# Top-k attention and a feed-forward block on one core: scores made two units ahead and set around the value products, loads spread, one transfer for the values

## The chip, the cores and the metric

The kernel runs on one core of a Trainium2 chip. The metric is the device time of one execution in microseconds (us); lower is better. The time of a kernel is the median of its runs. A profile shows one execution, on five engines: PE (TensorE, matrix products and transposes; its weight loads are listed as PEld), DVE (VectorE), ACT (ScalarE), POOL (GpSimd) and SP (SyncE, which issues nearly all transfers here). Each engine works through its own list of instructions in order.

## The reference

For 8 batches and 8 heads, 576 queries and keys of 64 numbers each, the 32 largest scores of each query are kept, and a softmax over them weighs the values. The heads are put side by side into rows of 512, and a block of layer norm, a hidden layer of 2048 with ReLU and a residual follows.

```python
scores = scale * np.matmul(q, k.transpose(0, 1, 3, 2))          # (8, 8, 576, 576)
kth = np.partition(scores, -top_k, axis=-1)[..., -top_k:-top_k + 1]
mask = scores >= kth
scores = np.where(mask, scores, -1000000000.0)
attn = np.exp(scores - np.max(scores, axis=-1, keepdims=True))
attn = attn / (np.sum(attn, axis=-1, keepdims=True) + 1e-09)
x = heads_side_by_side(np.matmul(attn, v))                      # (8, 576, 512)
xn = (x - mu) / np.sqrt(var + 1e-06) * g_ln
out = x + np.maximum(xn @ w_ch1, 0.0) @ w_ch2                   # 512 -> 2048 -> 512
```

Everything is float32, but the weights come as float64 and are turned into float32 on the chip.

## The kernel before

**Jobs, groups, units.** A job is a pair of heads of one batch with some of their query tiles; a unit is one tile of 128 queries for both heads (two tiles of scores, 128x576 each), or, for the last 64 queries, one "rest" unit that holds both heads in one tile. There are 160 units, counted from 0. Batch 0 has jobs of two units and then four jobs with the rest unit alone (units 0 to 19); batch 1 has four jobs of two and four of three (20 to 39). From batch 2 on, each batch has 20 units: four jobs of three units (two tiles and the rest unit) and then four jobs of two. So jobs of three end with units 42, 45, 48, 51, then 62, 65 and so on, jobs of two with 53, 55, 57, 59, then 73 and so on. The four jobs of three are the first of their heads in the batch: they load q and k and turn them. The jobs of two fetch the turned tiles that were kept in HBM.

**Steps.** All instructions are issued in the order in which one loop writes them down (`for n in range(END)`, one step for each unit); nothing reorders them. In step n, with n above 8:

- `scores(x)` (L386 on PE, evacuated by ACT, L367) for the units that `due(n)` names: n+1 up to step 16, both in step 17, n+2 after that. Their tile `sc` has 5 buffers.
- `values(g)` (L600, L607): the value products of a group whose last unit is n-3. They need `pt`, the turned weights (one buffer), the values `vb`, and a tile `ends` for the 64 keys of each head that do not fill a block of 128.
- `select(u, 0)` to `select(u, 3)` on DVE: four rounds of finding the 8 largest (L421, L429) and taking them out (L415); between the second and the third stand `halve` of unit n+1 (L407, L408), which needs its scores, and in some steps `turn_heads` (L316).
- `prepare` and `watch` of unit n-1 on POOL (L452, L444, L445): the threshold.
- `mask` of unit n-1: ACT (L481), then a subtraction on POOL (L484). `weigh` of unit n-2: the exponential on ACT (L492), the first of the two ahead of the step's copies of scores.
- The weights of unit n-2 are turned into `pt`: by PE (L546, L575), or, from unit 40 on for every unit that is neither a rest unit nor the last of its group, by `move`: two transposes on DVE (L524), a store `turned` to HBM (L529) and four loads into `pt` (L532), which wait for the store's landing. `move` stands at the very end of the step, after `select(u, 3)`.
- `load_values`, near the end of the step after a job's last unit: four transfers on SP, two into `vb` (L301) and two into `ends` (L305). `ends` are two tiles, zeroed once, for jobs in turn.
- `load`, right after `turn_heads`: eight transfers of q and k on SP (L289) in one go.
- `fill()`, eight times in a step, puts in products of the feed-forward block (L745, L902), as many as an even share over the steps asks for; it counts a tick that the class `Later` uses to put work off.

Tiles for scores, turned weights, value products and other brief results share five PSUM buffers of one pool (`brief`, tag "ps").

```python
        ahead = [] if n == 0 else [n + 1] if n < CONVERTING else [n + 2]
        if n == CONVERTING:
            ahead = [n + 1, n + 2]
        return [units[i] for i in ahead if i < N]
```

Of the kernel before, what the change touches and what calls it, by code (L numbers as in the profile page):

```python
# [11 lines left out]
FP32 = mybir.dt.float32  # L12
# [9 lines left out]
J = 4  # L22
# [7 lines left out]
def compute(  # L30
# [12 lines left out]
    nc = tc.nc  # L43
    P = nc.NUM_PARTITIONS
    B, H, S, D = q.shape
# [3 lines left out]
    JP = J * P  # L49
    R = S - JP  # L50
# [6 lines left out]
    def pool(name, bufs, **kw):  # L57
        return ctx.enter_context(tc.tile_pool(name=name, bufs=bufs, **kw))

    NV = 2  # L60
# [6 lines left out]
    vpool = pool("v", NV)  # L67
# [23 lines left out]
    def const(shape, name):  # L91
        return consts.tile(shape, FP32, tag=name, name=name)
# [9 lines left out]
        return mmps.tile([P, 512], FP32, tag="mm", name=name)  # L102


    ends = [const([P, P], f"ends{i}") for i in range(NV)]
    for t in ends:
        nc.gpsimd.memset(t[:], 0.0)
    if doubt is not None:
        watched = const([P, 34], "watched")
        nc.gpsimd.memset(watched[:], -1.0)  # L110
# [88 lines left out]
    queue = list(pieces)  # L199
# [5 lines left out]
    def weights(n, phase):  # L205

        now, before = batches.get(n, []), batches.get(n - 1, [])
        if phase == 0:  # L210
            for x in batches.get(n + 1, []):
                x.fetch()
            for x in now[0::2]:
                x.split()
        elif phase == 1:
            for x in before:
                x.join()
            for x in now[1::2]:
                x.split()
# [10 lines left out]
    def pop():  # L230
        kind, cost, run, may = todo.pop(0)
        assert not may or may()
        owed[0] -= cost
        run()
# [24 lines left out]

    sums_later, ends_later, stores = Later(), Later(), Later()  # L260

    def fill(least=0):
        tick[0] += 1
        ends_later.settle(END_AGE)
        fetch_forms(FETCH_AGE)
        owed[0] = min(owed[0] + share[0], 6.0)
        while todo and (not todo[0][3] or todo[0][3]()):
            if owed[0] < todo[0][1] / 2 and least <= 0:
                break
            least -= 1  # L270
            pop()
# [7 lines left out]
            self.b, self.hp = b, hp  # L279
            self.groups = groups  # L280

    def load(job, first, second):

        job.ins = {}
        for name, src, queue in (("k", k, first), ("q", q, second)):
            t = ldpool.tile([P, S], FP32, tag=name + "in", name=name + "in")
            for i in range(P // 32):
                head, d0 = 2 * job.hp + i * 32 // D, i * 32 % D
                queue.dma_start(  # L289
                    t[i * 32 : (i + 1) * 32, :].rearrange("b (n a) -> b n a", a=32),  # L290
                    src[job.b, head, :, d0 : d0 + 32].rearrange("(n b) a -> b n a", b=32),
                )
            job.ins[name] = t

    def load_values(job):
        vb = vpool.tile([P, 2 * J, D], FP32, tag="v", name="vb")
        job.ends = ends[jobs.index(job) % NV]
        for hh in range(2):
            rows = v[job.b, 2 * job.hp + hh]
            k0, end = (0, JP) if hh == 0 else (R, 0)  # L300
            nc.sync.dma_start(  # L301
                vb[:, hh * J : (hh + 1) * J, :],
                rows[k0 : k0 + JP, :].rearrange("(c p) d -> p c d", p=P),
            )
            nc.sync.dma_start(  # L305
                job.ends[hh * R : (hh + 1) * R, hh * D : (hh + 1) * D],
                rows[end : end + R, :],
            )
        job.v = vb

    def turn_heads(job):
        job.T = {}
# [48 lines left out]
    def scores(u):  # L361

        u.sc = scpool.tile([P, 2, S], FP32, tag="sc", name="sc")
        made = [score_half(u, s) for s in range(2)]
        for t in range(len(u.tiles)):
            for s in range(2):
                nc.scalar.copy(  # L367
                    u.sc[:, t, s * HALF : (s + 1) * HALF], made[s][t][:, 0:HALF]
                )
# [148 lines left out]
    def move(u):  # L518

        i0 = place_of(u)  # L520
        ni = P // 32
        blocks = u.sc[:].rearrange("p t n -> p (t n)")[:, 0 : 2 * JP]
        for t in range(2):
            nc.vector.transpose(  # L524
                blocks.rearrange("p (j t c n) -> p j t c n", j=ni, t=2, c=J)[:, :, t],
                u.e[:, t, t * R : t * R + JP].rearrange("p (c j k) -> p j c k", c=J, k=32),
            )
        hbm = hbmpool.tile([P, 2 * JP], FP32, tag="turned", name="turned")
        nc.sync.dma_start(hbm[:], blocks)  # L529
        for j in range(ni):  # L530
            to = u.group.pt[j * 32 : (j + 1) * 32, 0 : 2 * J].rearrange("k c n -> k (c n)")
            nc.sync.dma_start(  # L532
                to[:, i0 * 2 * P : (i0 + ni) * 2 * P].rearrange("k (i x) -> k i x", i=ni),
                hbm[:, j * 2 * P : (j + 1) * 2 * P].rearrange("(i k) x -> k i x", k=32),
            )
# [59 lines left out]
    def values(g):  # L595
        vb = g.job.v
        av = brief("av")
        for c in range(J):
            for h in range(2):
                nc.tensor.matmul(  # L600
                    av[h * D : (h + 1) * D, 0 : g.nq],
                    vb[:, h * J + c, :],
                    g.blocks[:, h, 0 : g.nq // 32, c, :],
                    start=(c == 0),
                    stop=False,
                )
        nc.tensor.matmul(  # L607
            av[:, 0 : g.nq], g.job.ends[:], g.pt[:, 2 * J, 0 : g.nq],
            start=False, stop=True,
        )  # L610
        g.av = av
# [316 lines left out]
            )  # L928

    PER_ROW = 1.71e-3  # L930
    SUM_AGE, END_AGE, FETCH_AGE, STORE_AGE = 7, 6, 10, 8
    blocks = []
    plain_done, formed, used, fetched = [None], [None], [], [0]

# [41 lines left out]
    def fetch_forms(age):  # L976
        if done(formed[0]):
            free = 4 + sum(tick[0] - x >= age for x in used)
            while fetched[0] < min(free, 8 * (len(blocks) - 1)):
                fetch_form()  # L980
# [11 lines left out]
    jobs = []  # L992
# [7 lines left out]
    units = []  # L1000
# [7 lines left out]
    N = len(units)  # L1008
    END = N + 6

    fresh = []
# [8 lines left out]
    CONVERTING = max(n for n in batches if batches[n]) + 2  # L1020
    EARLY = jobs[NHP].first
# [16 lines left out]
    for j in jobs:  # L1038
        if j.hp == NHP - 1:
            b = j.b  # L1040
            step = j.last + (3 if j.last < EARLY else 4)
# [28 lines left out]
    def after(n):  # L1070

        turned = at(n - 1) if n - 1 < EARLY else at(n - 2) if n - 2 >= EARLY else None
        last = at(n - 2) if n - 2 < EARLY else at(n - 3) if n - 3 >= EARLY else None
        return turned, last.group if last and last is last.group.units[-1] else None

    def due(n):

        ahead = [] if n == 0 else [n + 1] if n < CONVERTING else [n + 2]  # L1080
        if n == CONVERTING:
            ahead = [n + 1, n + 2]
        return [units[i] for i in ahead if i < N]

    DVE_UNIT = 6.0 + 1.65 * low_rounds
    DVE_REST, DVE_MOVE, DVE_TURN = 0.58 * DVE_UNIT, 1.4, 1.45
# [3 lines left out]
    for j in jobs[1:]:  # L1090
        before = jobs[jobs.index(j) - 1]
        made = next(n for n in range(N) if units[j.first] in due(n))
        step = min(before.first, made - 1)
        if j.twin:
            fetches.setdefault(max(step - 1, 0), []).append(j)
        else:
            turns[step] = j
            keeps[step + 1] = j
# [43 lines left out]
                    left += sum(b.cost() for b in gives[m])  # L1142
        return max(0.0, even) / SLOTS

    recips, rows_of = {}, {}
    pairs_left, made_pair = list(range(4)), []

    def arrived(n, key, x):
# [19 lines left out]
    for n in range(END):  # L1168
# [9 lines left out]
        ex, g = after(n)  # L1178
        g = g if g and not g.quick else None
# [7 lines left out]
        moved = ex is not None and ex.moved  # L1187

        if ex and not early:
            weigh(ex, 0)  # L1190
        for x in due(n):
            scores(x)
        if g:
            values(g)
        if u:
            select(u, 0)
        for j in fetches.get(n, []):
# [40 lines left out]
        if n in turns:  # L1238
            turn_heads(turns[n])
            later = fresh.index(turns[n]) + 1  # L1240
            if later < len(fresh):
                load(fresh[later], nc.sync, nc.sync)
        if not quick:
            weights(n, 1)
        fill()
        if mk and not early:
            mask(mk, 0)
# [9 lines left out]
            select(u, 2)  # L1257
        for blk, i in rows_of.pop(n, []):
            blk.stats(i)
        for blk in gives.get(n - 2, []):  # L1260
            blk.inverse()
        if last and ex.group.sums is not None:
# [12 lines left out]
        for x in (u if n < EARLY else None, mk if n > EARLY else None):  # L1275
            if x and x is units[x.job.last]:
                load_values(x.job)
        if quick:

            values(quick)  # L1280
            take_values(quick)
            for den in recips.pop(n + 1):
                nc.vector.reciprocal(den, den)
            place(quick)
            weights(n, 0)
            weights(n, 1)
        if u:
            select(u, 3)
            if u.i < CONVERTING:
                prepare(u)  # L1290
        if moved:
            move(ex)
        for x in (g, quick):
            if x and x.job.hp == NHP - 1:
                for qt in x.qts:
# [7 lines left out]
        if late and late.job.hp == NHP - 1:  # L1303
            r = late.job.b // 2
# [62 lines left out]
```

## Time and profile before

| | |
|---|---|
| median of 3 runs | 1657.19 us (1655.44 to 1660.09) |
| the profiled execution | 1655.4 us, of it 1653.6 us span of instructions |
| PE, DVE, ACT, POOL busy | 1508.0, 1334.3, 1067.4, 1078.1 us |
| granted clock of PE, mean | 0.963 of full speed |
| transfers | 211.5 MB, mean 128 GB/s |

The profile gives the busy time of each engine and its share of the span, the span in 40 slices of 41 us (each digit is the busy share in tenths, 9 for 90% or more; PEclk is the clock granted to PE in tenths), groups of instructions by line with their durations, and for idle time the instruction that ended it ("waited for"). "L386" is a line of the kernel before; the sequencer of SP is listed as SPq. A wait for several things is put down to the one that came last by the profile, and with transfers that share a semaphore the name can be that of a neighbour in the queue. The stretches of the batches: up to about 340 us the weights are converted and batches 0 and 1 run, then come the other batches, and from about 1500 us on only feed-forward products are left.

### The profile page before, as it was taken

To read this page: it belongs to the slowest core of one execution; us is meant where nothing else is said; L and a number is where in the kernel's file an instruction comes from. 1 tells how busy PE (TensorE), PEld (TensorE's weight loads), DVE (VectorE), ACT (ScalarE), POOL (GpSimd) and SP (SyncE) were. 2 spreads that over 40 slices of the span, in tenths; PEclk is the share of its full clock that TensorE was granted. 3 is DMA by queue.
4 is the path that set the end of the run, shared out by engine and by line. 5 is a ranking of instruction groups with operands and counts; after the bars stand their busy time and mean duration, and the time that the engine had idled before them with its cause. 6 is when DMAs were issued, how large, how long until landed. Compare 5 with 4: busy or idle time off the path is not lost. (4 is left out here: it accounts for less than half of the span.)

```text
span 1653.6 us, 27426 instructions
## 1 busy us (share of the span) xinstructions
PE 1508.0 (91%) x7898; PEld 1132.7 (68%) x7898; DVE 1334.3 (81%) x3990; ACT 1067.4 (65%) x2712; POOL 1078.1 (65%) x1607
## 2 busy tenths in 40 slices
PE   2557898999989899899999999999989999999997
PEld 1235546677757677677777776677767777778886
DVE  6878998788989898899998988799879999884000
ACT  5777966677757676567666765677656766654311
POOL 4667866867657475667675866576756676856433
PEclk9768999999989999999999999999999999999999
DMA  7433434321454354554655444545554445442211
GB/s 199 110 100 114 130 81 119 114 66 46 109 167 152 109 168 118 162 153 118 185 160 168 126 126 135 163 138 138 158 158 150 134 135 181 149 131 71 91 32 53
DMA packets 358951, 211.52 MB, mean 128 GB/s; under 512 B 250756, under 2 KB 331144, under 8 KB 358792
## 3 DMA queue, kind: packets, MB, share of 16 engines
q1 hardware_dynamic: 354056, 209.10, 43.8%
q8 instruction: 65, 1.06, 0.3%
q10 hardware_dynamic: 4736, 0.59, 0.2%
q14 instruction: 94, 0.77, 0.2%
HBM read 145.62 MB, written 63.96 MB: 127 GB/s over the span
## 5 line engine op out<-in xcount | busy, mean ns | idle before, releaser
L484 POOL TENSOR_TENSOR e<-e,sc 128x576 f32<-128x576 f32 x288 | 412.4, 1435 | 419.4 <-ACT e L481 403.1
L745 PE MATMUL hps<-xT,w 128*128 128x256 f32 x2304 | 548.2, 384 | 2.5 <-ACT xT L707 2.5
L745 PEld LDWEIGHTS hps<-xT,w 128*128 128x128 f32 x2304 | 422.0, 191 | 72.8 <-issue 16.7
L429 DVE MAX8 m<-hi 128x8 f32<-128x296 f32 (+1 forms) x1152 | 464.3, 444 | 1.1
L415 DVE MATCH_REPLACE8 hi<-m,hi 128x288 f32<-128x288 f32 (+1 forms) x864 | 378.2, 444 | 0.0
L902 PE MATMUL ops<-w,h 128*128 128x256 f32 x1360 | 324.8, 381 | 0.0
L902 PEld LDWEIGHTS ops<-w,h 128*128 128x128 f32 x1360 | 247.7, 190 | 40.4 <-issue 6.9
L492 ACT ACTIVATE e<-e,m 128x576 f32<-128x576 f32 x288 | 224.8, 780 | 52.8 <-POOL e L484 52.4
L407 DVE TENSOR_TENSOR hi<-sc 128x576 f32<-128x576 f32 (+1 forms) x160 | 120.1, 751 | 157.4 <-POOL watched L452 135.7
L481 ACT ACTIVATE e<-sc,m 128x576 f32<-128x576 f32 x288 | 223.9, 781 | 14.6 <-POOL m L444 13.9
L367 ACT COPY sc<-scps 128x288 f32<-128x288 f32 x576 | 195.1, 406 | 38.6 <-PE scps L386 18.3
L600 PE MATMUL av<-pt,vb 128*64 128x256 f32 (+2 forms) x1088 | 159.4, 439 | 37.7 <-DMA pt<-turned 18.2
L768 ACT ACTIVATE h<-hps 128x512 f32<-128x512 f32 x144 | 86.5, 601 | 103.7 <-PE hps L745 102.9
L600 PEld LDWEIGHTS av<-pt,vb 128*64 128x64 f32 x1088 | 80.2, 149 | 106.5 <-issue 50.3
L386 PE MATMUL scps<-kT,late_qT 64*128 64x288 f32 (+3 forms) x832 | 129.0, 413 | 5.3 <-ACT pt L558 3.2
L902 PE MATMUL ops<-wt,s 128*128 128x256 f32 x544 | 129.2, 381 | 0.0
L546 PE MATMUL tp<-ident,e 128*128 128x128 f32 x576 | 93.9, 289 | 37.8 <-ACT e L492 37.4
L386 PE MATMUL scps<-kT,qT 64*128 64x288 f32 x512 | 94.8, 471 | 29.5 <-ACT sign L168 11.8
L408 DVE TENSOR_TENSOR lo<-sc 128x576 f32<-128x576 f32 (+1 forms) x160 | 120.9, 756 | 0.0
L546 PEld LDWEIGHTS tp<-ident,e 128*128 128x128 f32 x576 | 73.9, 148 | 65.7 <-ACT e L492 51.6
L421 DVE MAX8 hi<-lo 128x8 f32<-128x288 f32 x288 | 118.0, 446 | 0.0
L386 PEld LDWEIGHTS scps<-kT,late_qT 64*128 64x128 f32 (+1 forms) x832 | 72.0, 168 | 59.4 <-issue 23.5
(106 smaller groups left out, 1905.9 us busy)
## 6 DMA issues: line engine op xcount, KB each, us to landing
turned<-sc SPq DMA_DIRECT2D x72, 512.0 KB, 2.6
pt<-turned SPq DMA_DIRECT2D x288, 128.0 KB, 2.7
w<-forms SPq DMA_DIRECT2D x136, 256.0 KB, 3.8
vb<-in_v_dram SPq DMA_DIRECT2D x136, 128.0 KB, 3.1
raw<-in_moe_w_ch_dram SPq DMA_DIRECT2D x32, 512.0 KB, 4.3
kT<-kept SPq DMA_DIRECT2D x36, 288.0 KB, 3.2
kin<-in_k_dram SPq DMA_DIRECT2D x128, 72.0 KB, 2.3
kept<-kT SPq DMA_DIRECT2D x32, 288.0 KB, 2.9
```

Source lines behind the costliest of these rows:

```text
L367: nc.scalar.copy(u.sc[:, t, s * HALF : (s + 1) * HALF], made[s][t][:, 0:HALF])
L386: nc.tensor.matmul(ps[i * R : i * R + ql, o : o + width], qT[r, q0 : q0 + ql], kT[r, k0 : k0 + width], start=True, stop=True,)
L408: nc.vector.tensor_tensor(lo, a, b, ALU.min)
L415: nc.vector.match_replace(x, m[:, t, :], x, LOWEST)
L429: nc.vector.max(m[:, t, :], u.hi[:, t, 0:width])
L481: nc.scalar.activation(u.e[:, t], u.sc[:, t], AF.Relu, bias=u.edge[:, t : t + 1], scale=-STEEP)
L484: nc.gpsimd.tensor_tensor(u.e[:, t], u.e[:, t], u.sc[:, t], ALU.subtract)
L492: nc.scalar.activation(u.e[:, t], u.e[:, t], AF.Exp, bias=u.bias[:, t : t + 1], scale=-scale, accum_out=g.den[:, col : col + 1],)
L546: nc.tensor.transpose(ps[:, c * P : (c + 1) * P], u.e[:, t, c * P + t * R : (c + 1) * P + t * R], ident[:],)
L600: nc.tensor.matmul(av[h * D : (h + 1) * D, 0 : g.nq], vb[:, h * J + c, :], g.blocks[:, h, 0 : g.nq // 32, c, :], start=(c == 0), stop=False,)
L745: nc.tensor.matmul(ps[0][:, side * N : (side + 1) * N], w1[:, c, f * P : (f + 1) * P], self.xT[:, c, 0:N], start=(c == 0), stop=(c == NC - 1),
L902: nc.tensor.matmul(bank[name][:, 0:Q], a(j), rhs, start=first and j == 0, stop=(j == G - 1), skip_group_check=not first,)
```

## The change

- `due(n)` names two units ahead from step 0 on. Where step n has value products and step n-1 has none, unit n+1 is scored in step n instead of in step n-1: the scores of n+1 stand ahead of the value products, those of n+2 behind them. In a step without value products that is followed by one with them, no scores are made.
- `load_values` issues one transfer for both heads' 1152 rows in nine blocks of 128. The middle block holds the last 64 keys of one head and the first 64 of the other; `fill_ends` copies its two halves into one single tile `ends`, on POOL, a step later, ahead of `mask(mk, 0)`.
- `load` puts its eight transfers off (from `EARLY` on, step 8): two with each tick, from the third tick on.
- `move(ex)` stands after `select(u, 2)` instead of after `select(u, 3)`, and so ahead of `load_values`.

```diff
-    ends = [const([P, P], f"ends{i}") for i in range(NV)]
-    for t in ends:
-        nc.gpsimd.memset(t[:], 0.0)
+    ends = const([P, P], "ends")
+    nc.gpsimd.memset(ends[:], 0.0)
...
     def fill(least=0):
         tick[0] += 1
+        loads.settle(LOAD_AGE)
...
-    def load(job, first, second):
+    def load(job, first, second, later=False):
...
+            for i in range(P // 32):
+                if later:
+                    age = (4 * len(job.ins) + i) // 2
+                    loads.add(lambda i=i, part=part: part(i), -age)
+                else:
+                    part(i)
...
     def load_values(job):
-        vb = vpool.tile([P, 2 * J, D], FP32, tag="v", name="vb")
-        job.ends = ends[jobs.index(job) % NV]
-        for hh in range(2):
-            rows = v[job.b, 2 * job.hp + hh]
-            k0, end = (0, JP) if hh == 0 else (R, 0)
-            nc.sync.dma_start(
-                vb[:, hh * J : (hh + 1) * J, :],
-                rows[k0 : k0 + JP, :].rearrange("(c p) d -> p c d", p=P),
-            )
-            nc.sync.dma_start(
-                job.ends[hh * R : (hh + 1) * R, hh * D : (hh + 1) * D],
-                rows[end : end + R, :],
-            )
-        job.v = vb
+        job.v = vpool.tile([P, 2 * J + 1, D], FP32, tag="v", name="vb")
+        rows = v[job.b, 2 * job.hp : 2 * job.hp + 2].rearrange("h s d -> (h s) d")
+        nc.sync.dma_start(job.v[:], rows.rearrange("(c p) d -> p c d", p=P))
+
+    def fill_ends(job):
+        for h in range(2):
+            r = slice(h * R, (h + 1) * R)
+            nc.gpsimd.tensor_copy(ends[r, h * D : (h + 1) * D], job.v[r, J, :])
...
-                    vb[:, h * J + c, :],
+                    vb[:, h * (J + 1) + c, :],
...
-            av[:, 0 : g.nq], g.job.ends[:], g.pt[:, 2 * J, 0 : g.nq],
+            av[:, 0 : g.nq], ends[:], g.pt[:, 2 * J, 0 : g.nq],
...
-    SUM_AGE, END_AGE, FETCH_AGE, STORE_AGE = 7, 6, 10, 8
+    SUM_AGE, END_AGE, FETCH_AGE, STORE_AGE, LOAD_AGE = 7, 6, 10, 8, 3
...
-        ahead = [] if n == 0 else [n + 1] if n < CONVERTING else [n + 2]
-        if n == CONVERTING:
-            ahead = [n + 1, n + 2]
-        return [units[i] for i in ahead if i < N]
+        def valued(n):
+            return n - 3 >= EARLY and after(n)[1] is not None
+
+        def held(n):
+            return not valued(n) and valued(n + 1)
+
+        return units[n + 1 : n + 2] * held(n - 1) + units[n + 2 : n + 3] * (not held(n))
...
-        step = min(before.first, made - 1)
+        step = max(min(before.first, made - 1), 0)
...
-        for x in due(n):
+        ahead = due(n) if n else []
+        for x in ahead[:1]:
             scores(x)
         if g:
             values(g)
+        for x in ahead[1:]:
+            scores(x)
...
-                load(fresh[later], nc.sync, nc.sync)
+                load(fresh[later], nc.sync, nc.sync, n >= EARLY)
+        if n == 0:
+            scores(units[2])
         if not quick:
             weights(n, 1)
+        if n in ends_due:
+            fill_ends(ends_due.pop(n))
...
         for blk, i in rows_of.pop(n, []):
             blk.stats(i)
+        if moved:
+            move(ex)
...
                 load_values(x.job)
+                ends_due[n + 1] = x.job
...
-        if moved:
-            move(ex)
```

More of the change, by code (lines that the diff above doesn't have):

```diff
@@ L260, in compute @@
     sums_later, ends_later, stores = Later(), Later(), Later()
+    loads = Later()
     def fill(least=0):
         tick[0] += 1
+        loads.settle(LOAD_AGE)
         ends_later.settle(END_AGE)
@@ L286, in load, with part @@
             t = ldpool.tile([P, S], FP32, tag=name + "in", name=name + "in")
-            for i in range(P // 32):
+            def part(i, t=t, src=src, queue=queue):
                 head, d0 = 2 * job.hp + i * 32 // D, i * 32 % D
@@ L1143, in slot @@
         return max(0.0, even) / SLOTS
-    recips, rows_of = {}, {}
+    recips, rows_of, ends_due = {}, {}, {}
     pairs_left, made_pair = list(range(4)), []
```

## The prediction

> **What bounds it now.** I read the busy times and the slices first, then who waited for whom, then the queue of SP around one wait, then one group of units in order of time.
>
> ```profile
> PE 1508.0 (91%) x7898; PEld 1132.7 (68%) x7898; DVE 1334.3 (81%) x3990; ACT 1067.4 (65%) x2712; POOL 1078.1 (65%) x1607
> ...
> PE   2557898999989899899999999999989999999997
> ...
> DVE  6878998788989898899998988799879999884000
> ...
> PEclk9768999999989999999999999999999999999999
> ```
>
> PE is the bound from 340 us to the end, and from 1520 us it works nearly alone. The matmuls do not change in number, so the time can fall only by PE's idle time, 1653.6 - 1508.0 = 146 us: by stretches of 40 us it is 94 us before 340, 42 us in 340 to 1480 and 10 us at the very end. DVE is close behind, mostly at 34 to 39 of 40 us. The waits of PE in 340:1480:
>
> ```profile
> PE av L600 <- DMA pt<-turned: 18.2, 7, 5.1
> PE av L600 <- DMA kept<-late_qT: 7.8, 2, 4.5
> PE av L600 <- DMA dr<-den: 6.0, 1, 6.0
> PE av L600 <- ACT pt L569: 3.4, 1, 3.4
> ```
>
> All stand before the value products and sum to 35.4 us. One of the 5 us waits ends at 489.8. SP just before it, in order of time (start, duration, issue, count):
>
> ```profile
> 475.09 2.97 SPq L289 DMA_DIRECT2D kin<-in_k_dram  x4
> 478.16 2.06 SPq L289 DMA_DIRECT2D qin<-in_q_dram  x4
> 480.27 0.50 SPq L301 DMA_DIRECT2D vb<-in_v_dram  x1
> ...
> 482.62 0.53 SPq L529 DMA_DIRECT2D turned<-sc  x1
> 485.45 1.75 SPq L532 DMA_DIRECT2D pt<-turned  x4
> ```
>
> The transposes of move() were done at 479.3; eight loads and four value transfers kept their store until 482.6, so pt landed at 489.6. Two stretches, one with such waits and one without (PE, PEld, DVE, ACT, POOL busy, then clock):
>
> ```profile
> 840.00:880.00 40.00, 39.31 (x210) 29.56 (x207) 34.39 (x105) 24.25 (x64) 28.74 (x49) 1.00 0.56 171
> 1000.00:1040.00 40.00, 33.20 (x161) 23.18 (x159) 28.41 (x82) 19.96 (x55) 22.59 (x38) 0.88 0.47 140
> ```
>
> **What the change takes away.** Spreading the loads takes up to eight issues of 0.5 us from ahead of move()'s store. One transfer for values for four saves 1.6 us of issues and stands behind move()'s five. move() ahead of select(u, 3) saves 0.74 us. So pt lands 3 to 5 us earlier, which alone would end nearly all of the 35.4 us.
>
> **What it adds: a wait on POOL.** fill_ends copies the two end blocks on POOL, and its first copy waits for the value transfer. With L the last unit of a job, the transfer is issued in step L+1, behind move() of unit L-1, and the copies stand in step L+2 directly ahead of the subtraction of unit L+1 (L484). Behind them wait both subtractions, watch and the two threshold scalings; ACT waits for the subtraction with the exponential of L+1 (L492), behind which stand the copies of the next scores; and of these, in a step with value products, the first are now unit L+4, which DVE halves in the same step. Before, those scores were copied a step earlier. One group before, from the DVE, POOL and ACT timelines:
>
> ```profile
> 838.47 1.29 DVE L524 STREAM_TRANSPOSE sc<-e 128x512 f32<-128x512 f32 x2
> 844.44 1.41 POOL L484 TENSOR_TENSOR e<-e,sc 128x576 f32<-128x576 f32 x1 [2.29 <-ACT e L481]
> 847.42 0.76 ACT L492 ACTIVATE e<-e,m 128x576 f32<-128x576 f32 x1
> 848.29 1.46 ACT L367 COPY sc<-scps 128x288 f32<-128x288 f32 x4
> 849.19 0.76 DVE L407 TENSOR_TENSOR hi<-sc 128x576 f32<-128x576 f32 x1 [0.30 <-POOL watched L452]
> ```
>
> New chain, from the end of the transposes: store issued, landed and four pt issues 4.55 us (4.57 is the median of the 72 moves in SP's timeline); value transfer V; two copies at 0.24 (the 128x64 copy of L633 takes 238 ns) with their hand-over 0.55; subtraction 1.41; exponential to the first copy 0.87; four copies 1.49; hand-overs 0.15. V is not in the trace. Rows on both sides:
>
> ```profile
> w<-forms SPq DMA_DIRECT2D x136, 256.0 KB, 3.8
> vb<-in_v_dram SPq DMA_DIRECT2D x136, 128.0 KB, 3.1
> raw<-in_moe_w_ch_dram SPq DMA_DIRECT2D x32, 512.0 KB, 4.3
> ```
>
> It moves 288 KB in runs of 256 B: not below 3.1, up to 4.3; I take 3.8, the row nearest in size. The chain is 12.8 us; where four spread loads still stand between pt and the values (16 of the 23 groups ahead of a three-unit group, by the program's order), 2.05 more: 14.85.
>
> The Trainium skill, page "DMA: Bandwidth & Descriptors", section "Anatomy of one DMA — SWDGE (gpsimd) path", fits a transfer of GpSimd's path as 2.0 us plus bytes over 436 GB/s. By it V would be an estimated 2.7 us and the sum below some 18 us less; but for the 128 KB transfer it gives 2.3 where the trace has 3.1.
>
> DVE does not take that long. From the transposes' end it has the last select 0.74 and the stretch 839.68 to 849.19 less the 0.30 it waited: 9.95 us. So it will idle 2.9 us, or 4.9 with loads, in every three-unit group. From that halving on, 849.19 to 853.25 and the next step to its transposes (3.83 selects, 1.34 halve, 1.61 select, 1.21 transposes) make 12.05, and 13.46 where turn_heads (1.41) is among them. The period of a three-unit group, transposes to transposes, becomes 28.3 (loads and turn), 26.9 (loads), 24.85 (neither). Against the periods read off the same line L524 before:
> - loads and turn, after L = 42, 62, 82, 102, 122, 142: 27.4, 27.8, 24.7, 30.8, 25.2, 24.6. Six times 28.3 is 9.3 us more. (Units are counted from 0 to 159.)
> - loads, L = 45, 65, 85, 105, 125: 27.3, 29.1, 25.3, 29.2, 31.6, the ones with the waits. Five times 26.9 is 8.0 less.
> - neither, L = 48 and every 20th: 22.3, 24.4, 26.6, 26.0, 25.7, 25.8; the last four have PE near 40 of 40 and stay: 3.0 more, and L = 145, 24.7, 0.2 more.
> - into a three-unit group, L = 59 to 139: 27.4, 28.8, 30.3, 29.3, 29.0, mostly PE's own pace: 0.9 more.
> - three units to two: 16.3 to 16.8, now 17.0: 2.7 more; two to two (17.7 and above): none.
>
> That is +8. Store and transfer take longer than their medians when form loads are in the queues (the store's landing 3.09 mean against 2.76, vb 3.5 against 3.1): 0.75 us in some 16 groups that the chain bounds is +12, of which I take half, since some of those already had a longer period. Main part: +14.
>
> **The rest.** Scores two ahead from step 0: halve waited for sc 3.65, 2.64, 3.65, 2.60 and 2.60 us between 71 and 122, 15.1 at most. But ACT paces these steps (31.8 of 40 us busy in 80:120, and PE waits 4.7 for ACT's e), and at 132.8 DVE waits for ACT's x anyway, where a lead is lost: -2, between -15 and +3 (an earlier turn could wait for kept). The copies' 33 us on POOL are hidden beside its 35% idle except in the chain. Scores on both sides of the products need nine turns of the five "ps" buffers: the second scores wait for ACT's copies of the first, covered by the 2.9 us of value products; without that cover 1 to 2 us in each of some 45 steps. One "ends" tile: the products of the job before are two steps back, no wait. Matmuls, PE's tail: none.
>
> Sum: 1655.4 (1653.6 span and 1.8 around it) + 14 - 2 = 1667.4. The median shown is 1657.2, 1.8 above that run, so 1669.
>
> **The clock.** The stretch with waits had 161 matmuls at 0.88 against 210 at 1.00, so a wait costs some 3 us beside itself. I count nothing for it: PE is not the bound in the groups that grow. The Trainium skill, "TensorE: Matmul & The Clock Gate", section "HAM oscillation", warns of idle gaps of PE above about 3.4 us, after which it runs at half rate. Five waits of 340:1480 are longer, and one such window at half rate each would make them an estimated 9 us dearer; by it that would come back where they go.
>
> **Rivals.**
> - *PE's waits go and PE stays the bound: faster.* The pt path really is 3 to 5 us shorter, and DVE idles 10% now, room for part of the stall. It would win if values land by 7 us after the transposes, or if the 2.9 and 4.9 us fall where DVE waits anyway (100 us for watched in 340:1480). With 10 of the 35.4 left over and 2 gained early it is 1655.4 - 25.4 - 2 + 1.8 = 1630. Against: the pt issues alone end at 4.55, and the smaller value transfer of now takes 3.1.
> - *Queues full: much slower.* At 530 the store took 7.5 us to land behind form loads. Three us more in 20 groups: 1730.
> - *They cancel:* within 5 us of 1657; 0.3% (about what a measurement can tell from no change) is 5 us.
>
> **Numbers.** Forecast (1662 to 1690) 0.47, faster rival 0.33, cancel 0.12, full queues 0.08. V at 3.1 takes 0.7 us off some 18 groups, and without congestion 6 more go: -19. V at 4.3 and all of the congestion add 9 and 6. The early part moves it by -13 to +5, and the second scores, uncovered in a third of their steps, by +20. The range reaches below the faster rival: 1622 to 1702. Slower is 0.47 and 0.08.
>
> **What would show it.** Right: POOL's idle time before the copies of "ends" about 5 us each, released by the value transfer, 200 us and more in all; DVE's halve waiting for ACT sc, 3 to 5 us in three-unit groups; PE's waits for pt nearly gone, but waits for POOL ends or ACT sc in their place. Wrong: POOL waiting under 2 us there; PE's idle time in 340:1480 under 25 us; early DVE waits gone with PE's idle before 340 under 85.

## The result and the profile after

The changed kernel takes 1730.35 us (median of 4 runs, 1725.44 to 1733.12) against 1657.83 us of the kernel before: a ratio of 1.0434, 95% interval 1.0402 to 1.0467. The prediction had the direction (slower) but said 1669 us, and the 1702 us at which its range ended is 28 us too low. The profiled execution has a span of 1731.3 us, 77.7 us more than before.

The page of the changed kernel: busy times, then the slices.

```profile
PE 1538.7 (89%) x7898; PEld 1151.7 (67%) x7898; DVE 1362.6 (79%) x3990; ACT 1072.0 (62%) x2712; POOL 1102.1 (64%) x1742
...
PE   3567888999888988899899998999899999999997
...
PEclk8568999999999999999999999999999999999999
```

The same 7898 matmuls are busy 30.7 us longer (1538.7 against 1508.0, at a mean granted clock of 0.947 against 0.963), and PE's idle time grew by 47.0 us, from 145.6 to 192.6. Those two make up the 77.7 us. Of PE's 40 slices 23 show a nine, against 29 before. The value products' largest waits on PE in 340:1560 (the same work takes longer now), and two waits of other engines in 340:1540 (us in total, times, longest):

```profile
PE av L605 <- DMA qin<-in_q_dram: 26.1, 6, 6.6
PE av L605 <- issue: 19.7, 7, 4.5
PE av L605 <- DMA kept<-kT: 8.7, 2, 5.3
PE av L605 <- DMA vb<-in_v_dram: 6.7, 4, 4.6
```
```profile
POOL ends L314 <- DMA vb<-in_v_dram: 185.4, 35, 11.5
DVE hi L412 <- ACT sc L372: 115.9, 33, 7.5
```

No wait for a load of `pt` is among the first four: that part did what was said. But the value products wait longer than before (68.2 us in all against 37.7). What they wait for goes by four names. The trace of one job shows that there it is the value transfer; group 3 of the experiments tests it for all. This is job L = 62, with the transposes of its last move ending at 652.9; SP, POOL, ACT, PE and DVE in order of time (start, duration, then the idle time before and what ended it):

```profile
652.94 0.35 SPq L534 DMA_DIRECT2D turned<-sc  x1
655.63 1.73 SPq L537 DMA_DIRECT2D pt<-turned  x4
657.41 0.97 SPq L292 DMA_DIRECT2D kin<-in_k_dram  x2
658.42 1.04 SPq L292 DMA_DIRECT2D qin<-in_q_dram  x2
659.56 0.45 SPq L309 DMA_DIRECT2D vb<-in_v_dram  x1
...
663.80 0.53 POOL L314 COPY ends<-vb 64x64 f32<-64x64 f32 x2 [8.62 <-DMA vb<-in_v_dram]
664.09 4.39 PE L605 MATMUL av<-pt,vb 128*64 128x320 f32 x16 [5.34 <-DMA kept<-kT]
665.84 0.78 ACT L497 ACTIVATE e<-e,m 128x576 f32<-128x576 f32 x1 [8.29 <-POOL e L489]
668.14 0.76 DVE L412 TENSOR_TENSOR hi<-sc 128x576 f32<-128x576 f32 x1 [5.19 <-ACT sc L372]
669.15 1.24 PE L391 MATMUL scps<-kT,qT 64*128 64x288 f32 x8
669.93 1.49 ACT L372 COPY sc<-scps 128x288 f32<-128x288 f32 x4 [1.90 <-PE scps L391]
```

The store is issued at once. In the kernel before it came 1.6 us after the transposes in this job, behind loads and values, and more than 2 us after them in 11 of the 72 moves; so the 3 to 5 us that the prediction took from ahead of it were there in few moves only. The value transfer now stands behind the store, its four `pt` issues and four loads, is issued 6.6 us after the transposes, and lands at 663.7. POOL's copies and PE's first product start within 0.4 us of that: both waited for the same transfer, for 8.62 and for 5.34 us. Behind POOL's copies stand subtraction, exponential, copies of scores and DVE's halving; behind PE's products the second scores (669.15), for which ACT waits again.

### The profile page after: what moved, and what is told of

It reads as the page before. It is cut to its first block, busy times and chain, and to the rows that moved or that the text cites. A ratio compares the mean times of both kernels' runs of the same rounds, so it can differ in the third digit from the quotient of the medians.

```text
span 1731.3 us, 27295 instructions
## 1 busy us (share of the span) xinstructions
PE 1538.7 (89%) x7898; PEld 1151.7 (67%) x7898; DVE 1362.6 (79%) x3990; ACT 1072.0 (62%) x2712; POOL 1102.1 (64%) x1742
## 4 chain that ended last, share of the span: by engine, by line
PE 46%; POOL 14%; DVE 12%; DMA 9%; ACT 8%; issue 6%; SPq 5%; DVEq 0%; POOLq 0%; ACTq 0%
PE hps L750 15%; PE ops L907 13%; POOL e L489 6%; PE av L605 6%; PE scps L391 6%; DMA turned<-sc 3%; DVE m L434 3%; DVE hi L420 3%; DMA vb<-in_v_dram 2%; SPq L292 2%; SPq L537 2%; ACT e L497 2%; PE tp L551 2%; DVE sc L529 2%; PE av L612 2%
## 5 line engine op out<-in xcount | busy, mean ns | idle before, releaser
L489 POOL TENSOR_TENSOR e<-e,sc 128x576 f32<-128x576 f32 x288 | 406.6, 1420 | 249.4 <-ACT e L486 225.0
L434 DVE MAX8 m<-hi 128x8 f32<-128x296 f32 (+1 forms) x1152 | 457.8, 443 | 0.2
L412 DVE TENSOR_TENSOR hi<-sc 128x576 f32<-128x576 f32 (+1 forms) x160 | 132.4, 827 | 201.8 <-ACT sc L372 135.1
L605 PE MATMUL av<-pt,vb 128*64 128x256 f32 (+2 forms) x1088 | 171.3, 465 | 68.2 <-DMA qin<-in_q_dram 26.1
L605 PEld LDWEIGHTS av<-pt,vb 128*64 128x64 f32 x1088 | 86.5, 157 | 142.7 <-issue 107.2
L314 POOL COPY ends<-vb 64x64 f32<-64x64 f32 x136 | 34.6, 254 | 213.4 <-DMA vb<-in_v_dram 187.7
L413 DVE TENSOR_TENSOR lo<-sc 128x576 f32<-128x576 f32 (+1 forms) x160 | 129.9, 812 | 0.0
L391 PE MATMUL scps<-kT,qT 64*128 64x288 f32 x512 | 98.8, 476 | 29.2 <-ACT sign L167 11.8
```

Source lines behind the costliest of these rows:

```text
L391: nc.tensor.matmul(ps[i * R : i * R + ql, o : o + width], qT[r, q0 : q0 + ql], kT[r, k0 : k0 + width], start=True, stop=True,)
L412: nc.vector.tensor_tensor(hi, a, b, ALU.max)
L434: nc.vector.max(m[:, t, :], u.hi[:, t, 0:width])
L489: nc.gpsimd.tensor_tensor(u.e[:, t], u.e[:, t], u.sc[:, t], ALU.subtract)
L605: nc.tensor.matmul(av[h * D : (h + 1) * D, 0 : g.nq], vb[:, h * (J + 1) + c, :], g.blocks[:, h, 0 : g.nq // 32, c, :], start=(c == 0), sto ...
```

## The experiments

Ratios are to the kernel before on the same chip. In five groups.

**1. Undoing one part each.** e1 has the four value transfers and two `ends` tiles of before, and no copies on POOL:

```diff
-        rows = v[job.b, 2 * job.hp : 2 * job.hp + 2].rearrange("h s d -> (h s) d")
-        nc.sync.dma_start(job.v[:], rows.rearrange("(c p) d -> p c d", p=P))
+        (four transfers into vb and ends, as before)
...
-            fill_ends(ends_due.pop(n))
```

> The changed kernel with the values as before: four transfers, two tiles of ends filled by the transfers, no copies on POOL. Order of the scores, spread loads and the earlier move stay. Theory A (a ring of two parts: POOL's wait for the value transfer delays the exponential of L+1, and the scores copied behind it are halved in the same step; it needs both parts): without the wait the ring is open, ACT's exponential is released within 1 us of its mask, and the time is 1645 to 1668 us, the 7 us of the early part included. Theory B (the order of the scores is enough: one unit is scored only in the step in which it is halved, and the second scores behind the value products hold ACT): 1700 us or more. Theory C (the wait on POOL is enough, whatever the order): 1640 to 1655.

e2 has the scores in the order of before, with the `due(n)` of before:

```diff
...
-        ahead = due(n) if n else []
-        for x in ahead[:1]:
+        for x in due(n):
             scores(x)
         if g:
             values(g)
-        for x in ahead[1:]:
-            scores(x)
```

> The changed kernel with the scores as before (all of a step's scores ahead of the value products, n+1 up to step 16 and n+2 after); the single value transfer and POOL's copies of the ends stay. Theory A: POOL still waits some 5 us for the transfer in each job, but the scores copied behind the late exponential are halved only a step later, about 9 us of slack, so DVE hardly waits for ACT's copies: 1640 to 1665 us. Theory B: 1635 to 1650. Theory C: the wait alone costs most of the 72 us, 1700 or more.

e3 has both, so only the spread loads and the early move are left.

> The changed kernel with both undone, so the kernel before with only the loads spread and the move ahead of the last select. All theories: the store no longer stands behind loads and value transfers, the 35 us of PE's waits before the value products go down to 10, and the time is 1625 to 1645 us. A rival: the waits come back elsewhere, 1650 to 1660.

Measured: e1 1694.72 us (1.0202 [1.0178, 1.0226]), e2 1700.12 us (1.0234 [1.0217, 1.0251]), e3 1656.32 us (0.9974 [0.9962, 0.9987]). Theory A, that the ring (the loop from one move's transposes to the next) needs both parts, fell: over e3 each alone costs some 40 us, and both together 76 us by the ratios (1.0434 and 0.9974), about the sum. B and C, which made one of them the whole, fell with it. e3 gains far less than the theories had it and came out where its rival was: its products wait for `vb` and `ends` 19.4 us, where they had waited for `pt`. In e2 the wait of POOL goes another way round to DVE, by `watch`, which stands behind the copies as well (DVE's wait for it before: 117.4, 52, 11.4 in this stretch):

```profile
POOL ends L314 <- DMA vb<-in_v_dram: 208.0, 41, 11.0
DVE hi L412 <- POOL watched L457: 162.4, 66, 7.2
```

**2. Moving the value transfer.** e4 issues it a step earlier, from unit 20 on; nothing else differs from the changed kernel:

```diff
...
-        for x in (u if n < EARLY else None, mk if n > EARLY else None):
+        for x in (u if n < EARLY or n >= LATE else None, mk if EARLY < n <= LATE else None):
             if x and x is units[x.job.last]:
                 load_values(x.job)
-                ends_due[n + 1] = x.job
+                ends_due[n + (2 if n >= LATE and x is u else 1)] = x.job
```

> The changed kernel with the value transfer issued a step earlier (in the step of a job's last unit, from unit 20 on), its copies of the ends where they were, in step L+2. The transfer then has a whole step more. Theory A: POOL's wait for it falls from 188 us to under 40, and the time to 1655 to 1680 us, of which 7 are the early part. Theory B: POOL's wait falls as well but the time stays above 1710. Theory C: 1650 to 1665.

e6 leaves it in its step, but directly ahead of the move:

```diff
+        if n > LATE and mk and mk is units[mk.job.last]:
+            load_values(mk.job)
+            ends_due[n + 1] = mk.job
         if moved:
             move(ex)
...
```

> The changed kernel with the value transfer issued directly ahead of the move of L-1 instead of behind it, in the same step (from unit 23 on): it needs no longer stand behind the move's five transfers, so it lands some 4 to 5 us earlier against the transposes. Theory D: POOL's wait falls by 4.5 us in each of some 40 jobs, from 185 us in 340:1540 to about 30, and the time to 1650 to 1675 us; the move itself is 0.5 us later. Rival: the whole step of the earlier try was needed, because PE and POOL run ahead: 1680 to 1710.

e15 puts the move back to the end of the step, behind the value transfer again.

> The changed kernel with the move back at the end of the step, behind the last select and so behind the value transfer again; everything else as changed. Theory D (all of the loss beyond the early part is the value transfer standing behind the move on SP): 1640 to 1655 us, as when the transfer was put ahead of the early move. Rival (the earlier place of the move pays and is needed to keep the weights early): 1660 to 1690.

Measured: e4 1646.51 us (0.9910 [0.9894, 0.9927]), e6 1645.13 us (0.9940 [0.9923, 0.9957]), e15 1664.77 us (1.0046 [1.0029, 1.0062]). All three take back most of the loss, and e4 and e6 are faster than any of their theories had it. In e6 the value transfer changes places on SP with the move and the loads between them, and by the ratios (1.0434 and 0.9940) 82 us go: what the change costs hangs on the value transfer standing behind them. e15 came out where its rival had it, that the early move is needed: with the move late the products wait for `pt` again (11.5 us in 340:1540, against 2.3 in e6), and the time stays 0.5% above the kernel before; with the values ahead of the early move it is 0.6% below.

**3. Who waits.** Three kernels leave every transfer where the change put it and only let PE or POOL read a constant tile in place of what it brings, so that the values are left out of the result in part or in whole. e17 frees PE (first edit), e18 frees POOL (second edit), e19 both:

```diff
-                    vb[:, h * (J + 1) + c, :],
+                    ident[:, h * D : (h + 1) * D],
...
-            av[:, 0 : g.nq], ends[:], g.pt
+            av[:, 0 : g.nq], ident[:], g.pt
```
```diff
-            nc.gpsimd.tensor_copy(ends[r, h * D : (h + 1) * D], job.v[r, J, :])
+            nc.gpsimd.tensor_copy(ends[r, h * D : (h + 1) * D], ident[r, 0:D])
```

> The changed kernel, but the value products read a constant tile instead of the values and ends (left out of the result: the values), so PE waits for pt alone; POOL still waits for the transfer and copies the ends. The sum of the prediction priced just this: if POOL's ring was sized right, some 1668 us, 12 over the kernel before. If POOL's wait carries about half of the loss, 1685 to 1700 us. If PE's wait is what counts, 1645 to 1655.

> The changed kernel, but POOL's copies of the ends read a constant tile (left out of the result: the 64 end rows of each head's values), so POOL does not wait; PE's products wait for the late transfer as changed, and the second scores behind them. If PE's wait carries about half of the loss: 1685 to 1700 us, like the kernel with the old four transfers behind the move (1694.7). If it was covered, as the prediction had it: 1645 to 1660.

> Both: products and copies read a constant tile (the values are left out of the result), the transfer is issued and lands as changed, behind the move. If only the two waits cost: at or a little under the kernel with the transfer a step earlier (1646.5), so 1638 to 1650 us. If the transfer's place in the queue or its traffic costs as well: 1660 or more.

Measured: e17 1739.80 us (1.0498 [1.0468, 1.0528]), e18 1712.61 us (1.0318 [1.0282, 1.0353]), e19 1641.21 us (0.9900 [0.9874, 0.9926]). When nobody waits, the late transfer costs nothing, and the change is worth 1%. So traffic and queue are not it. That the constant tile itself makes e19 fast is not it either: e4 and e6 read the real values in time and have nearly the same ratio (0.9910 and 0.9940). But each wait alone costs nearly the whole (99 and 71 us above e19; both together 89), not half as was expected: they lie side by side, and taking one away lets the other do its work. Why POOL's wait alone comes out even 0.6% dearer than both was not settled. How POOL's wait reaches PE when PE does not wait for values is in the waits of e17, 340:1540:

```profile
POOL ends L314 <- DMA vb<-in_v_dram: 185.4, 38, 10.3
PEld scps L391 <- ACT sc L372: 72.5, 40, 5.3
PE scps L391 <- ACT sc L372: 54.5, 25, 4.7
```

The second scores need buffers that ACT's copies of the first free; those copies stand behind the exponential that waits for POOL. PE waits 54.5 us there (3.2 in the changed kernel). How PE's wait reaches DVE when POOL does not wait is in the waits of e18:

```profile
ACT sc L372 <- PE scps L391: 184.2, 64, 11.9
DVE sc L529 <- ACT e L497: 86.1, 27, 8.3
```

ACT waits for the second scores, the exponential of the next tile behind them is late, and DVE's transposes for the next move wait for that.

**4. The second scores by themselves.** e5 sets both units' scores ahead of the products:

```diff
-        ahead = due(n) if n else []
-        for x in ahead[:1]:
+        for x in due(n) if n else []:
             scores(x)
         if g:
             values(g)
-        for x in ahead[1:]:
-            scores(x)
```

> The changed kernel with both units' scores ahead of the value products (which units a step scores stays as changed). Theory D (the value transfer, issued behind the move, is late, and whatever stands behind its two users pays: subtraction and exponential behind POOL's copies, scores behind PE's products): scores are out of reach of PE's wait, POOL's wait is not, so the time comes down to about that of the old order, 1695 to 1712 us, ACT's wait for scores from 53 us to under 15. Theory S (the hold alone, one unit scored only in the step in which it is halved, is what costs): no change, 1720 to 1735.

Measured: 1841.49 us (1.1131 [1.1108, 1.1155]), far outside what either theory said. PE in its job L = 62:

```profile
685.46 1.72 PE L391 MATMUL scps<-kT,qT 64*128 64x288 f32 x10
695.56 2.28 PE L391 MATMUL scps<-kT,qT 64*128 64x288 f32 x6 [8.38 <-ACT sc L372]
697.77 3.33 PE L605 MATMUL av<-pt,vb 128*64 128x320 f32 x16
```

After ten of sixteen score products the buffers are used up, and PE stands until ACT's exponential, which waits for POOL (8.72 us, to 694.21), has let the copies through. Products that had cover before them now stand behind the whole chain. So with five buffers the second scores are cheaper behind the products than ahead of them, although e18 shows that they have a price there too.

**5. What the parts are worth with values in time.** e7 is e4 with the scores in the old order; e14 is e7 with the eight loads in one go; e9 is the kernel before with its four value transfers a step earlier and nothing else; e12 is e9 with loads spread and the early move; e16 is the kernel before with the early move alone.

The edit of e14 on top of e7:

```diff
-                load(fresh[later], nc.sync, nc.sync, n >= EARLY)
+                load(fresh[later], nc.sync, nc.sync)
```

> The kernel with the value transfer a step earlier, and the scores in the order of before. It tells what the order of the scores is worth once values are there in time. If the order pays (DVE waited 40 us for watched with it against 111 without, when values were early or loaded the old way): slower than with the new order, 1650 to 1658 us. If it only costs (7 us early, scores behind products): 1636 to 1644.

> The kernel with one value transfer a step earlier and the scores in the old order (1629.5 us), but with the eight loads in one go as before. It tells what the spreading is worth: the store then stands behind up to eight loads again in some 11 jobs, 3 us each of PE's wait: 1636 to 1648 us. Rival (values out of the way are enough): 1626 to 1632.

> The kernel before with one edit: its four value transfers are issued a step earlier (from unit 20 on), so they no longer stand ahead of the move's store; the eight loads still do. Theory D: PE's waits before the value products fall from 35 to some 15 us, those at steps with eight loads stay: 1640 to 1650 us. Rival (PE's waits were hidden by DVE's pace all along): 1653 to 1660.

> The kernel before with three edits: four value transfers a step earlier, loads spread, the move ahead of the last select. Against the kernel before with only the values earlier (1635.8 us) it takes the eight loads from ahead of the store: PE's waits for pt, 11 us there, go to under 3: 1620 to 1632 us. Rival (DVE's pace takes over): 1632 to 1640.

> The kernel before with one edit: the move goes ahead of the last select, and so ahead of the four value transfers. Theory D: pt lands 2.3 us earlier, the values some 5 to 6 us later, and with the old order only PE's products wait for them: between 1652 and 1672 us, PE's waits before the products now for vb and ends. Rival (as predicted, the store's earlier issue counts): 1640 to 1650.

| kernel | us | ratio, 95% interval |
|---|---|---|
| e7: values early, one transfer, old order | 1629.52 | 0.9855 [0.9830, 0.9880] |
| e14: the same, loads in one go | 1638.13 | 0.9883 [0.9862, 0.9904] |
| e9: before, values early | 1635.82 | 0.9878 [0.9857, 0.9898] |
| e12: before, values early, loads spread, move early | 1632.03 | 0.9845 [0.9822, 0.9868] |
| e16: before, move early | 1646.92 | 0.9927 [0.9905, 0.9949] |

e7 and e12 beat both kernels, by 1.5% and, against the changed kernel, by some 100 us. The values a step earlier are the larger part of it (e9: more than either theory said). The early move alone is worth 0.7%, as its rival had it: behind it the values are late, but in the old order and without copies on POOL only PE's products wait for them. e12 came out where its two expectations meet. With the loads spread on top (e3) most of that is gone again, although the products of e3 wait no longer for the values than those of e16 (19.4 us against 23.6); why, stays open. One transfer with POOL's copies, or four without, makes no difference (e7, e12). The new order costs with values in time too (e4 against e7: 0.9910 and 0.9855). Spreading the loads gained some 0.3% with values early (e14 against e7), but the intervals overlap.

## Why the prediction was wrong

The mechanism was named: value transfer behind the move, POOL's copies waiting for it, exponential, copies, halving. The size came out six times too small (72.5 us where 12 were forecast). The table has periods in us (means): from the end of the transposes of a job's last move to that of the next job's, in brackets how many there are; "predicted" is what the prediction's sums give for each kind, and "nobody waits" is e19:

| group | before | predicted | after | nobody waits |
|---|---|---|---|---|
| loads and turn (6) | 26.75 | 28.3 | 31.10 | 25.54 |
| loads (5) | 28.50 | 26.9 | 29.45 | 26.00 |
| neither (7) | 25.06 | 25.5 | 26.04 | 25.17 |
| into a three-unit group (5) | 28.97 | 29.2 | 31.28 | 28.03 |
| three to two (6) | 16.53 | 17.0 | 18.77 | 16.99 |
| two to two (18) | 20.66 | 20.66 | 21.12 | 20.77 |

Weighted by their numbers these periods grew by 71.0 us, where the prediction had 8, and 14 with half of its congestion. The other 6.7 us of the 77.7 were there at unit 42, ahead of them. By the steps of the prediction:

- *The chain to the halving:* right. Predicted 12.8 and 14.85 us, measured, from the transposes to the halving, 12.81 (neither) and 15.45 (both kinds with loads). The transfer, estimated at 3.8 us, has a median of 3.8:

```profile
vb<-in_v_dram SPq DMA_DIRECT2D x68, 288.0 KB, 3.8
```

  The estimate by the Trainium skill's page "DMA: Bandwidth & Descriptors", section "Anatomy of one DMA — SWDGE (gpsimd) path", 2.7 us by a fit that the page gives for GpSimd's path, was too short by 1.1 us for this transfer of SyncE.
- *The rest of the ring, from the halving to the next transposes, 12.05 and 13.46 us:* this step failed. It was added up from DVE's instructions without a gap, so that a longer wait for the halving was partly made good in the rest. The rest measured 13.23 (neither), 14.00 (loads) and 15.65 (loads and turn). Even in e19 it is 14.27, 14.61 and 15.21: there the halving comes at 10.3 to 11.4 us after the transposes, and the rest has PE's pace. In the order loads and turn, loads, neither, a halving that is 5.1, 4.05 and 1.9 us later than in e19 lengthens the period by 5.6, 3.4 and 0.9: with loads little is made good, without them half. e17 is the very case that the prediction's sum priced, POOL's wait alone: 1739.8 us where the sum had 1669, with the halving at 14.97, 15.73 and 12.62 us and periods of 30.78, 30.35 and 25.87. PE's wait has a way of its own into the periods: in e18 the halving is not late (10.50, 11.42 and 10.84), and they are 30.86, 30.44 and 25.95.

  The sentence "PE is not the bound in the groups that grow" is the error behind it. PE is busy nearly throughout with nobody waiting, and nearly was before (PE, PEld, DVE, ACT, POOL busy, then clock; before, changed, e19):

```profile
340.00:1540.00 1200.00, 1157.63 (x6201) 884.51 (x6198) 1049.21 (x3165) 791.67 (x2066) 793.25 (x1269) 0.98 0.47 137
340.00:1540.00 1200.00, 1112.25 (x5840) 837.58 (x5838) 1030.17 (x3061) 763.10 (x1995) 767.06 (x1295) 0.97 0.46 131
340.00:1540.00 1200.00, 1169.15 (x6300) 892.98 (x6299) 1074.23 (x3186) 803.50 (x2096) 816.37 (x1380) 1.00 0.48 137
```

  An engine busy 1169 of 1200 us has little room to catch up; most of what DVE or ACT withholds from it is time. DVE is nearly as full in the kind that grew most: of the 25.5 us of "loads and turn" in e19, PE works 24.6 and DVE 24.0. In the changed kernel that period is 5.6 us longer, 3.6 of it idle time of PE and 2.0 longer busy time. The comparison with the periods before hid this, since those held waits for `pt` that the change took away: the true base is not 1657 but the 1641 of e19.
- *"Second scores ... covered by the 2.9 us of value products":* failed, in both ways that it left out. The products themselves wait for the values, and the second scores behind them (e18); and where the products don't wait, the second scores do (e17). The prediction had 1 to 2 us in a third of 45 steps, some 20 us, at the end of its range. Either wait alone makes 70 us or more over e19.
- *The clock, counted as nothing:* failed. Of the 91.3 us between the spans of e19 and the changed kernel, 34.2 are busy time of as many matmuls of the same shapes (1538.7 against 1504.5). Times the mean granted clock, 0.947 and 0.970, both are some 1458 us, so the lower clock accounts for it. The prediction had seen that a wait costs some 3 us beside itself, and then left it out.
- *Early part, -2 us:* the lead of 3 to 5 us of units 5 to 9 came and was lost, as said; but at unit 20 the halving is 6 us late, and it stays so (6.7 at unit 42). Without the new values and their single `ends` tile it is 4.4 us late at unit 21 (e1), with the old order 2.5 (e2). "The products of the job before are two steps back, no wait" does not hold for jobs of a single unit, where POOL's copies wait for them at 236, 245 and 259 us:

```profile
POOL ends L314 <- PE av L612: 10.2, 3, 6.7
```

- *Congestion, +6:* the size was about right. The chain without loads shows none (12.81 us against 12.8); the one with loads is 0.6 us longer than summed, some 7 us in 11 groups.
- *The rivals:* that PE's waits go and come back as nothing is what e19 shows without the waits, at 1641 where the rival had 1630. "Queues full" had the number, 1730, but not the cause. What was missing was the rival that PE stands at the same transfer as POOL, and that either wait costs PE nearly the whole. The signs named for POOL and DVE came true (185.4 and 115.9 us in the rows above, 5.3 and 3.5 each); for PE the prediction expected waits for POOL's `ends` or ACT's `sc`, and the transfer itself stood there.

## What to carry to other kernels

When a transfer is pushed back in a queue, list everyone who waits for it and what stands behind each of them in order, not only the longest chain; two waits side by side each cost nearly the whole here (e17, e18), so taking one away showed little. Price a ring against the engine that is full: where it had next to no slack within a period, most of the time by which its input was late was added here, with the longer busy time at a lower clock. And before a step is moved in front of another, look at the queue that both use: here the place of one transfer on SP, ahead of a move or behind it, was worth 82 us.

## What the runs showed of the hardware

The clock after a wait of PE, in the job shown above (PE, PEld, DVE, ACT, POOL busy, then granted clock):

```profile
660.00:664.00 4.00, 0.00 (x0) 0.00 (x0) 2.89 (x10) 0.00 (x0) 0.20 (x1) 0.67 0.97 221
664.00:669.00 5.00, 4.91 (x18) 2.22 (x18) 0.86 (x2) 2.17 (x6) 3.58 (x7) 0.58 0.09 25
```

For 5 us after the wait of 5.34 us the granted clock was 0.58, and sixteen products took 4.39 us; they take 2.37 where the wait before them was 1.39, 2.60 or even 3.38 us (starting at 725.22, 895.17 and 472.08 in the changed kernel). They took 4.06 us after a wait of 2.79 us (753.27), and 3.50 after one of 2.54 in e19. The Trainium skill, "TensorE: Matmul & The Clock Gate", section "HAM oscillation — how this bites in real kernels", puts the limit at gaps of about 3.4 us. The clock near half rate after 5.34 us agrees, but slower products followed shorter waits here too, and below 3.4 us the length of the wait alone does not tell which will be slow.
